# An adaLN attention block on one core: opening rebuilt around early loads and norms, and units of values placed between halves of the key products

## The chip, the cores and the metric
The kernel runs on one core of one Trainium2 chip. The metric is device time in microseconds (us), the median of the runs shown. The core has a matrix engine (PE, its weight loads shown as PEld), a vector engine (DVE), an activation engine (ACT), a general engine (POOL), a queue engine (SP) that issues nearly all transfers, and 16 DMA engines.

## The reference
One adaptive layer-norm block on x of 2048 rows by 512, all float32: attention with 32 heads of 16, then a Mish feed-forward of width 1792.

```python
mod = (_silu(c) @ w_mod).reshape(c.shape[0], 6, 1, -1)
sa, ca, ga, sb, cb, gb = (mod[:, 0], mod[:, 1], ...)
h = _layernorm(x) * (1 + ca) + sa
x = x + ga * _A_ref(h, A_wqkv, A_wo)      # softmax attention, 32 heads
h = _layernorm(x) * (1 + cb) + sb
x = x + gb * _B_ref(h, B_w1, B_b1, B_w2)  # dense, mish, dense
```

What this change touches is the way to the first `h` and to keys, queries and values: x is normalised, scaled by `1 + ca` and shifted by `sa`, and multiplied by `wqkv`.

## The kernel before
The order of all engines is written out by hand. Every product is made of three: each operand is split into a high part (rounded to the matrix engine's fast float32 form) and a low part (the rest), and high by high, high by low and low by high are added up in PSUM. `hi_copy` makes the high part, `lo_sub` the low one.

The work falls into an opening, four blocks of early projections, a lead-in of 20 steps, 512 steps of attention (32 groups of four heads and 512 queries, 16 steps each), with the feed-forward of earlier rows beside them, and a tail.

- Opening. SP loads c, the first two slices of the modulation weights (`wma`, shift and scale, 1 MB each), four tiles of x (128 rows each), the first 128 columns of the key and query weights (`wr`), then the rest of x and the value weights. POOL fills constants. `sil` is silu(c). Sums over c are matrix products whose left operand is `sil`, one slice of 128 rows to a strip of 32 output rows; a second product with `sel` adds the four strips and turns them into columns (`modc`). `first_norm` takes mean and variance of x tiles 0 to 3 on DVE and the root on POOL; `first_apply` normalises them; `first_tr` transposes them on PE into four PSUM banks.
- Blocks. A block `tb` is 512 rows. `stats_tb` (DVE, POOL) and `apply_tb` (ACT) normalise its four tiles, `tr_tb` transposes them and makes, for each of four k, `h_h` (ACT, high part), `hf` (DVE, full value, after ACT has read the bank) and `h_l` (the difference: on DVE for the k in `LOV[tb]`, else on POOL). The first key product (`qk_unit(1, 0, tb)`) starts with eight products on `h_h` ("early") and ends with four on `h_l` ("late"); block 0 has the query product too. Its result is split by ACT (`qh`) and DVE (`ql`) and stored. In blocks 1 and 2, all eight early products are followed by two units of values (`v_unit`: 12 products of 256 columns for 128 rows); then come block `tb + 1`'s transposes of two k, the late products, and the transposes of the other two.
- Banks. PSUM has a ring of six banks and two more (`ms`, `acc`). `ring()` hands out the next bank; whoever writes it waits for those that read its former contents.
- Lead-in. Step t from -20 to -1 takes two pairs of maxima (`max_pair`: four products of 64 rows on `ka` and `qa`, two DVE reductions of 1024) and then as many products of the queue of units as `CREDIT` allows; one credit is one product of 512 columns. `plan` lists the units: values of the first half, then query and key projections. What is left at step 0 goes beside the scores.

One PE queue, one DVE queue and so on run strictly in the order written.

## Time and profile before

| | us |
|---|---|
| median of 3 runs | 1693.89 (1693.4 to 1694.09) |
| profiled execution | 1694.02 |
| its span | 1692.1 |
| busy PE / DVE / ACT / POOL | 1671.4 / 1442.0 / 1354.5 / 821.1 |
| first x tile ready (start of its statistics) | 9.76 |
| first product of block 0 (PE, L131) | 19.95 |
| first maxima (lead-in starts) | 50.29 |
| first score (step 0) | 103.31 |

Times inside the execution are from the start of the span. A timeline row has start, duration, engine, line, operation, tiles (written, then read), shapes, count, and in brackets the idle time before it and what ended it. A stretch row has its length, then for each engine busy us and, as (x…), the instructions, then the granted PE clock (1.00 is full), the DMA share and GB/s. Rows with one count over several instructions merge them.

### The profile page before, as it was taken

To read this page: it belongs to the slowest core of one execution; us is meant where nothing else is said; L and a number is where in the kernel's file an instruction comes from. 1 tells how busy PE (TensorE), PEld (TensorE's weight loads), DVE (VectorE), ACT (ScalarE), POOL (GpSimd) and SP (SyncE) were. 2 spreads that over 40 slices of the span, in tenths; PEclk is the share of its full clock that TensorE was granted. 3 is DMA by queue.
4 is the path that set the end of the run, shared out by engine and by line. 5 is a ranking of instruction groups with operands and counts; after the bars stand their busy time and mean duration, and the time that the engine had idled before them with its cause. 6 is when DMAs were issued, how large, how long until landed. Compare 5 with 4: busy or idle time off the path is not lost.

```text
span 1692.1 us, 33739 instructions
## 1 busy us (share of the span) xinstructions
PE 1671.4 (99%) x12410; PEld 925.8 (55%) x12410; DVE 1442.0 (85%) x2371; ACT 1354.5 (80%) x2610; POOL 821.1 (49%) x843
## 2 busy tenths in 40 slices
PE   7999999999999999999999999999999999999999
PEld 5755665555444555555555455555555455555587
DVE  8888888888889888888889888888889888884377
ACT  6257777777778988888888998888888998888674
POOL 7556224665413564555323564555323565555443
PEclk9999999999999999999999999999999999999999
DMA  7877545777755343434355434424354533533261
GB/s 250 260 239 201 132 136 179 229 224 216 216 172 142 106 101 84 127 80 131 85 145 148 118 74 97 137 73 132 82 146 126 131 93 77 143 107 128 77 230 63
DMA packets 114029, 238.44 MB, mean 141 GB/s; under 512 B 23824, under 2 KB 49424, under 8 KB 107912
## 3 DMA queue, kind: packets, MB, share of 16 engines
q1 hardware_dynamic: 113864, 236.28, 49.5%
q8 instruction: 98, 1.61, 0.4%
q14 instruction: 67, 0.55, 0.1%
HBM read 179.95 MB, written 51.44 MB: 137 GB/s over the span
## 4 chain that ended last, share of the span: by engine, by line
PE 92%; DVE 3%; ACT 3%; DMA 1%; issue 1%; POOL 1%; SPq 0%; ACTq 0%; DVEq 0%; POOLq 0%
PE bk L605 29%; PE ring L587 22%; PE ring L538 20%; PE bk L138 10%; PE bk L131 3%; PE ring L131 2%; PE ring L1214 2%; DVE mx L540 2%; ACT pr L590 1%; PE ring L552 1%; DMA xt<-in_A_x 0%; PE ring L917 0%; PE ring L567 0%; PE ring L138 0%; DMA ka<-kscr 0%
## 5 line engine op out<-in xcount | busy, mean ns | idle before, releaser
L540 DVE TENSOR_REDUCE mx<-ring 128x1 f32<-128x512 f32 x1968 | 1222.9, 683 | 151.3 <-PE ring L538 137.9
L590 ACT ACTIVATE pr<-ring 128x512 f32<-128x512 f32 x2048 | 1078.3, 603 | 209.3 <-PE bk L138 116.4
L538 PE MATMUL ring<-ka,qa 64*128 64x512 f32 x1968 | 818.6, 429 | 1.3 <-ACT pr L590 1.1
L587 PE MATMUL ring<-qa,ka 64*128 64x512 f32 x2048 | 759.4, 402 | 2.2 <-ACT pr L590 2.0
L605 PE MATMUL bk<-pr,vg 128*32 128x512 f32 x4096 | 545.1, 605 | 0.0
L538 PEld LDWEIGHTS ring<-ka,qa 64*128 64x128 f32 x1968 | 350.8, 184 | 326.2 <-DVE mx L540 251.3
L587 PEld LDWEIGHTS ring<-qa,ka 64*128 64x128 f32 x2048 | 374.0, 184 | 193.1 <-DVE mx L540 112.2
L138 PE MATMUL bk<-h,w 64*128 64x512 f32 (+1 forms) x1080 | 278.1, 391 | 0.0
L138 PE MATMUL bk<-w,a_h 64*128 64x512 f32 x632 | 211.0, 413 | 0.0
L138 PEld LDWEIGHTS bk<-h,w 64*128 64x128 f32 x1080 | 178.8, 185 | 8.4 <-ACT pr L590 1.5
L605 PEld LDWEIGHTS bk<-pr,vg 128*32 128x32 f32 x4096 | 80.8, 108 | 136.1 <-issue 126.6
L138 PE MATMUL bk<-w,a_l 64*128 64x512 f32 x316 | 124.3, 393 | 0.0
L138 PEld LDWEIGHTS bk<-w,a_h 64*128 64x128 f32 x632 | 106.9, 185 | 3.9 <-ACT hb L795 0.8
L973 POOL TENSOR_TENSOR y<-yd,y 128x512 f32<-128x512 f32 x44 | 56.9, 1292 | 89.1 <-ACT yd L972 84.2
L807 POOL TENSOR_SCALAR qq<-ee 128x512 f32<-128x512 f32 x25 | 15.5, 619 | 169.3 <-ACT ee L801 169.3
L823 POOL TENSOR_TENSOR qq<-qq,rr 128x512 f32<-128x512 f32 x42 | 54.2, 1289 | 86.0 <-ACT rr L817 86.0
L809 POOL TENSOR_TENSOR hb<-hb,ee 128x512 f32<-128x512 f32 x42 | 54.1, 1289 | 79.6 <-DVE ee L805 77.7
L138 PE MATMUL bk<-w,o_hl 64*128 64x512 f32 x288 | 79.1, 405 | 0.0
L100 POOL TENSOR_TENSOR a_l<-hb,a_h 128x512 fp32r<-128x512 f32 x53 | 73.2, 1381 | 4.4
L138 PEld LDWEIGHTS bk<-w,a_l 64*128 64x128 f32 x316 | 58.4, 185 | 3.2
L97 POOL TENSOR_SCALAR qh<-qf 128x512 fp32r<-128x512 f32 x27 | 16.7, 620 | 88.9 <-ACT qf L261 75.2
L138 PE MATMUL bk<-h_h,wl 64*128 64x512 f32 x168 | 57.2, 420 | 0.2 <-ACT pr L590 0.2
(222 smaller groups left out, 1917.0 us busy)
## 6 DMA issues: line engine op xcount, KB each, us to landing
ka<-kscr SPq DMA_DIRECT2D x124, 384.0 KB
w<-w2scr SPq DMA_DIRECT2D x56, 512.0 KB
w<-w1scr SPq DMA_DIRECT2D x46, 512.0 KB
vg<-vscr SPq DMA_DIRECT2D x32, 552.0 KB
qa<-qscr SPq DMA_DIRECT2D x124, 100.0 KB
kscr<-qh SPq DMA_DIRECT2D x16, 512.0 KB
qscr<-qh SPq DMA_DIRECT2D x32, 256.0 KB
w2scr<-hl SPq DMA_DIRECT2D x14, 512.0 KB
```

The source lines that it names most:

```text
L100: (nc.gpsimd if eng == "p" else nc.vector).tensor_sub(lo, src, hi.bitcast(F32))
L131: nc.tensor.matmul(acc, l, r, start=start, stop=stop)
L138: i = nc.tensor.matmul(acc, l[64 * g:64 * g + 64], r[64 * g:64 * g + 64], start=start and not then, stop=bool(stop and then))
L538: nc.tensor.matmul(pm, qt[64 * s:64 * s + 64, qs * P:(qs + 1) * P], kt[64 * s:64 * s + 64, kb * TB:(kb + 1) * TB], start=True, stop=True)
L540: nc.vector.tensor_reduce(out=mxs[n][:, s, 4 * j + qs, kb:kb + 1], in_=pm, op=ALU.max, axis=AX.X)
L587: nc.tensor.matmul(p_, kt[64 * s:64 * s + 64, kc * P:(kc + 1) * P], qt[64 * s:64 * s + 64, :], start=True, stop=True)
L590: e = nc.scalar.activation(pr, p_, AF.Exp, scale=SCALE)
L605: nc.tensor.matmul(accs[n][32 * h:32 * h + 32, :], vgs[n][:, o:o + 32], pts.pop((t, h)), start=(kc == 0), stop=(kc == 15))
L809: (nc.vector if tail else nc.gpsimd).tensor_mul(hb, hb, ee)
L823: nc.gpsimd.tensor_mul(qq, qq, rr)
L973: nc.gpsimd.tensor_add(y[i], yd, y[i])
L1214: nc.tensor.matmul(po[i // 2][:, i % 2, :], l[:, s], w[:, r, :], start=(f == 0 and j == 0), stop=(f == FT - 1 and j == 2))
```

## The change
Loads: c comes by ACT's queue, ahead of ACT's table load. SP loads x tiles 0 to 3, the shift's weights in four slices, x tiles 4 to 7, key weights, the scale's weights in four slices, query and value weights, the rest. POOL no longer fills the two `ka` tiles with ones; ACT copies them. `sel` is gone.

Opening: the statistics and applies of tiles 0 to 7 stand ahead of block 0, in pairs; tile 3 is applied on POOL, the rest on ACT. The sums run slice by slice, in an output of 32 equal rows per 128 columns, and one transpose turns a copy of it into columns. 66 transposes of the identity into an unused bank (`keep_busy`) stand among them. DVE makes the low part of the key weights and the high part of the query weights, and POOL the low part of the latter.

Blocks: in blocks 1 to 3 the early key products come in two halves, each followed by one unit of values, so six units instead of four are done here. `plan` starts at unit 6, and `CREDIT` is 6.65 instead of 7.2.

```diff
-    CREDIT = 7.2
+    CREDIT = 6.65
...
+    nc.scalar.dma_start(cc, c.rearrange("o (k p) -> p (o k)", p=P))
     nc.scalar.preload_act_table_set("natural_log_exp_and_others")
...
-        wma = [lp.tile([P, DK, D], F32, name=f"wma{i}") for i in range(2)]
-        for i in range(2):
-            nc.sync.dma_start(wma[i], w_mod[:, i * D:(i + 1) * D].rearrange("(k p) m -> p k m", p=P))
+        wma = [[lp.tile([P, D], F32, name=f"wma{i}{k}") for k in range(DK)] for i in range(2)]
+
+        def load_mod(i):
+            for k in range(DK):
+                nc.sync.dma_start(wma[i][k], w_mod[k * P:(k + 1) * P, i * D:(i + 1) * D])
+
         for t in range(4):
             load_x(t)
-        slice_load(1, 0, lp, lp)
-        slice_load(0, 0, lp, lp)
+        load_mod(0)
         for t in range(4, 8):
             load_x(t)
+        slice_load(1, 0, lp, lp)
+        load_mod(1)
+        slice_load(0, 0, lp, lp)
         slice_load(2, 0)
...
-        for i in range(2):
-            nc.gpsimd.memset(ka[i].bitcast(F32), 1.0)
+        hi_copy("a", ka[0], ones.to_broadcast([P, S]))
+
+        spare = ring()
+
+        def keep_busy(n):
+            for _ in range(n):
+                nc.tensor.transpose(spare[:, :P], ident, ident)
+
+        keep_busy(40)
...
+        def mod_sums(i, ks):
+            for k in ks:
+                for m in range(DK):
+                    nc.tensor.matmul(prs[i][32 * m:32 * m + 32, :P], sil[:, k:k + 1].to_broadcast([P, 32]),
+                                     wma[i][k][:, m * P:(m + 1) * P], start=(k == 0), stop=(k == DK - 1))
+
+        def mod_cols(i):
+            row = lp.tile([P, P], F32, name=f"row{i}")
+            nc.vector.tensor_copy(row, prs[i][:, :P])
+            nc.tensor.transpose(prs[i][:, P:2 * P], row, ident)
+            cols = prs[i][:, P:2 * P:32]
+            if i:
+                nc.vector.tensor_scalar_add(modc[:, i, :], cols, 1.0)
+            else:
+                nc.vector.tensor_copy(modc[:, i, :], cols)
...
+        for q in range(2):
+            stats_two(q)
+        first_apply(3, "p")
+        for q in range(2, 4):
+            stats_two(q)
+        mod_sums(0, (0, 1))
+        keep_busy(6)
+        first_apply(0)
+        first_tr(0)
+        mod_sums(0, (2,))
+        first_apply(1)
+        first_tr(1)
+        mod_sums(0, (3,))
+        first_apply(2)
+        first_tr(2)
+        first_tr(3)
+        keep_busy(12)
+        mod_cols(0)
+        hi_k = split_hi(1, 0, "a")
+        for i in range(4, 8):
+            first_apply(i)
+        for k in range(DK):
+            mod_sums(1, (k,))
+            keep_busy(1)
+        mod_cols(1)
+        split_lo(1, 0, hi_k, "v")
+        hi_q = split_hi(0, 0, "v")
+        split_lo(0, 0, hi_q, "p")
+        keep_busy(4)
+        tr_tb(0, pts=pts)
...
-            pe_queue.extend(m for e in early for m in e)
-            pe_run()
-            if tb in (1, 2):
-                for kc in (2 * tb - 2, 2 * tb - 1):
-                    unit(v_unit(0, kc, "ring"))
+                pe_queue.extend(m for e in early for m in e)
+                pe_run()
+            else:
+                for i in range(2):
+                    pe_queue.extend(early[0][j + k] for k in (2 * i, 2 * i + 1) for j in (0, DK))
+                    pe_run()
+                    unit(v_unit(0, 2 * tb - 2 + i, "ring"))
...
-    plan = [(-PRO, 2, 0, range(4, 16)), (-PRO, 0, 1, (0,)), (-PRO, 1, 1, range(NB)), (-PRO, 1, 2, range(NB)),
+    plan = [(-PRO, 2, 0, range(6, 16)), (-PRO, 0, 1, (0,)), (-PRO, 1, 1, range(NB)), (-PRO, 1, 2, range(NB)),
```

DVE's queue between the statistics and the first `hf` of block 0, before (the apply of tile 3, the columns, four pairs of statistics of block 1, of which the first and last stand here, and the first `hf`):

```order
L419 TENSOR_SCALAR xt_140<-xt_140,ln_rs4_189 128x512
L462 TENSOR_SCALAR modc_95<-bk_212 128x4
L463 COPY modc_95<-bk_212 128x4
L373 BN_STATS ln_st_247<-xt_146 128x6
L374 BN_AGGR ln_mv4_245<-ln_st_247 128x2
...
L373 BN_STATS ln_st_256<-xt_152 128x6
L374 BN_AGGR ln_mv4_245<-ln_st_256 128x2
L440 TENSOR_SCALAR hf_281<-ring_100,modc_95 128x512
```

and in the changed kernel, from the last statistics of block 1 on:

```order
L399 BN_STATS ln_st_278<-xt_150 128x6
L400 BN_AGGR ln_mv2_273<-ln_st_278 128x2
L439 COPY row0_338<-ring_96 128x128
L445 COPY modc_91<-ring_96 128x4
L439 COPY row1_368<-ring_96 128x128
L443 TENSOR_SCALAR modc_91<-ring_96 128x4
L98 TENSOR_TENSOR wl_372<-wr_152,wh_342 128x512
L93 CAST wh_374<-wr_158 128x512
L458 TENSOR_SCALAR hf_382<-ring_96,modc_91 128x512
```

The statistics of block 1 stand ahead of the columns now, and behind the columns stand two splits of weights.

PE's queue in block 1 before (`wh` on the right of the arrow first: values; `h_h` first: key products):

```order
L131 MATMUL ring_100<-h_h_117,wh_200 128x512 x4
L131 MATMUL ring_100<-h_h_117,wl_235 128x512 x4
L131 MATMUL ring_100<-wh_325,h_h_117 128x256 x4
L131 MATMUL ring_100<-wl_326,h_h_117 128x256 x4
L131 MATMUL ring_100<-wh_325,h_l_118 128x256 x4
```

and in the changed kernel, from the last product of the first half:

```order
L129 MATMUL ring_96<-h_h_113,wl_372 128x512
L129 MATMUL ring_96<-wh_422,h_h_113 128x256 x4
L129 MATMUL ring_96<-wl_423,h_h_113 128x256 x4
L129 MATMUL ring_96<-wh_422,h_l_114 128x256 x4
L129 MATMUL ring_96<-h_h_113,wh_342 128x512
```

The first unit of values has moved ahead of the last four early products.

SP's queue at the start before (c, the two slices of modulation weights, x):

```order
L331 DMA cc_128<-in_c 128x4x1
L341 DMA wma0_130<-in_w_mod 128x4x512
L341 DMA wma1_131<-in_w_mod 128x4x512
L336 DMA xt_134<-in_A_x 128x512
L336 DMA xt_136<-in_A_x 128x512
```

and in the changed kernel, from the last tile of the first four on:

```order
L332 DMA xt_138<-in_A_x 128x512
L339 DMA wma00_124<-in_w_mod 128x512
...
L332 DMA xt_150<-in_A_x 128x512
L231 DMA wr_152<-in_A_wqkv 128x4x128
L339 DMA wma10_128<-in_w_mod 128x512
L339 DMA wma11_129<-in_w_mod 128x512
L339 DMA wma12_130<-in_w_mod 128x512
```

x now leads, and the scale's weights stand behind eight tiles of x.

More of the change, by code (lines that the diff above doesn't have):

```diff
@@ L74, in adaln_block @@
     nc.gpsimd.memset(ones, 1.0)
-    sel = cst.tile([P, 1], F32, name="sel")
-    nc.gpsimd.memset(sel, 0.0)
-    for k in range(DK):
-        nc.gpsimd.memset(sel[32 * k:32 * k + 1, :], 1.0)
     lows = cst.tile([P, 1], F32, name="lows")
@@ L329, in adaln_block @@
         lp = es.enter_context(tc.tile_pool(name="lp", bufs=1))
-        cc = lp.tile([P, DK], F32, name="cc")
-        nc.sync.dma_start(cc, c.rearrange("o (k p) -> p (o k)", p=P))
         xts = []
@@ L363, in adaln_block @@
         nc.vector.tensor_mul(sil, cc, e)
+        hi_copy("a", ka[1], ones.to_broadcast([P, S]))
         rss = {}
@@ L441, in tr_tb @@
                 lo_sub("v" if k in LOV[tb] else "p", h_l[:, k, s], hf, h_h[:, k, s])
[L443 to L466 removed]
+        for q in range(2):
[19 more added lines that the diff above has]
+            first_apply(i)
+        for k in range(DK):
+            mod_sums(1, (k,))
[6 more added lines that the diff above has]
+        tr_tb(0, pts=pts)
         def constants():
```

85 lines of the change are left out of this document (27 added, 58 removed).

## The prediction
> **What bounds the kernel now.** I read the stretches of the span first, then the timeline of the opening.
>
> ```profile
> core 0: us, PE busy (x) PEld busy (x) DVE busy (x) ACT busy (x) POOL busy (x), PEclk, DMA share, GB/s
> 0.00:16.20 16.20, 7.00 (x32) 4.02 (x33) 10.47 (x14) 5.30 (x8) 12.14 (x36) 1.00 0.91 317
> 16.20:50.29 34.09, 31.64 (x174) 25.15 (x175) 30.75 (x53) 24.17 (x37) 21.29 (x25) 1.00 0.66 218
> 50.29:56.83 6.54, 6.54 (x38) 5.42 (x38) 4.95 (x5) 1.85 (x4) 5.21 (x4) 0.74 0.62 224
> 56.83:103.31 46.48, 46.36 (x263) 32.57 (x262) 42.81 (x40) 7.97 (x19) 24.66 (x25) 1.00 0.90 278
> 103.31:1588.00 1484.69, 1479.57 (x11428) 778.30 (x11429) 1276.51 (x2155) 1258.42 (x2456) 720.92 (x716) 1.00 0.49 132
> ```
>
> From 103.31, where the first scores start, PE is busy 1479.57 of 1484.69 us, and no row of the change lies behind that point except one product; the order of every engine there is the old one. So the change is worth what it moves the moment 103.31. Ahead of it lie three stages: loads and norms (to 16.2, PE mostly waiting), four blocks of early projections (to 50.29, DVE busy 30.75 of 34.09) and 20 lead-in steps of maxima and units (to 103.31, PE full).
>
> ```profile
> 1.23 1.04 SPq L341 DMA_DIRECT2D wma<-in_w_mod  x2
> 2.31 2.14 SPq L336 DMA_DIRECT2D xt<-in_A_x  x4
> 3.18 5.55 DVE L361 TENSOR_SCALAR sil_e<-sil_e 128x4 f32<-128x4 f32 x1 [1.53 <-ACT sil_e L360]
> 9.76 0.69 DVE L394 BATCH_NORM_STATS2 ln_st<-xt 128x6 f32<-128x512 f32 x1 [0.61 <-DMA xt<-in_A_x]
> 11.21 0.59 ACT L452 COPY row<-ring 128x512 f32<-128x512 f32 x1 [8.05 <-PE ring L448]
> 12.91 0.59 ACT L452 COPY row<-ring 128x512 f32<-128x512 f32 x1 [1.12 <-PE ring L448]
> 16.54 0.15 DVE L463 COPY modc<-bk 128x4 f32<-128x4 f32 x1
> 16.61 0.68 DVE L373 BATCH_NORM_STATS2 ln_st<-xt 128x6 f32<-128x512 f32 x1
> 19.84 0.81 DVE L440 TENSOR_SCALAR hf<-ring,modc 128x512 f32<-128x512 f32 x1
> 21.40 0.69 DVE L100 TENSOR_TENSOR h_l<-hf,h_h 128x512 fp32r<-128x512 f32 x1
> 22.11 3.78 POOL L100 TENSOR_TENSOR h_l<-hf,h_h 128x512 fp32r<-128x512 f32 x3
> 22.19 2.93 ACT L384 ACTIVATE xt<-xt,ln_rs 128x512 f32<-128x512 f32 x4 [0.38 <-POOL ln_rs L378]
> 27.78 0.81 DVE L440 TENSOR_SCALAR hf<-ring,modc 128x512 f32<-128x512 f32 x1
> ```
>
> The first x tile waits behind 2 MB of modulation weights until 9.76. The modulation columns are there at 16.7, but DVE then takes statistics of block 1 and reaches the first `hf` at 19.84; block 1's first `hf` comes 7.94 us later.
>
> **Loads and norms.** x goes first. The last slice of modulation weights is then the 17th piece of 256 KB where the first x tile was the 9th. Pieces come at the rate of this row:
>
> ```profile
> 9.20:20.00 10.80, 10.63 (x49) 7.33 (x49) 7.94 (x20) 4.79 (x8) 5.75 (x12) 1.00 1.07 395
> 25.03 1.03 ACT L93 CAST wh<-wr 128x1024 fp32r<-128x1024 f32 x1
> 15.00 2.68 POOL L100 TENSOR_TENSOR wl<-wr,wh 128x512 fp32r<-128x512 f32 x2
> 15.07 1.47 DVE L419 TENSOR_SCALAR xt<-xt,ln_rs 128x512 f32<-128x512 f32 x1 [2.02 <-POOL ln_rs L399]
> ```
>
> Eight more pieces are 2.1 MB, 5.3 us at 395 GB/s; the queue starts 0.5 us earlier: 9.7 + 5.3 - 0.5 = 14.5. Then a sum, 0.4 (a quarter of the 12.91 less 11.21 that a sum of all four slices took), a copy, 0.3 (between 0.15 and 0.59), a transpose, 0.3, and an add, 0.15: columns at 15.7, by these bounds 15.3 to 16.2.
>
> What I cost at nothing: eight weight loads for two add six issues on SP, which stay beside data that is slower (a piece takes 0.66 us); without that cover each costs its issue, some 0.5. c on ACT's queue adds an issue there, and the two fills of `ka` come from POOL, some 2 us each (twice the 1.03 us row). Both lie inside the 8.05 us in which ACT waited; behind them stand only Exp and the first applies. Without that cover the columns stay and the applies come up to 4 us later. POOL without the fills frees DVE, which stood 5.55 us at 3.18, so `sil` no longer comes at 9.14. The apply of the fourth tile on POOL takes at most a POOL subtraction's 1.3 us, before 12, with POOL's norm chains of tiles 4 to 7 behind it and these due only at 15.7. The sums with `sel` go and 66 transposes come, on a PE that had 7.00 busy of 16.20.
>
> The statistics of block 1 took 3.2 us (16.61 to 19.84). They and their applies are now done by 15.7, since twelve pieces are in by 9.7 + 2.0 - 0.5 = 11.2. So DVE goes from the columns to the key weights' low part (0.69, as the `h_l` row) and the query weights' high part (0.45, between 0.15 and 0.69) and starts `hf` at 16.9, 2.9 us ahead of 19.84. The 2.93 us of ACT at 22.19 leave the block, where DVE and not ACT is late.
>
> Part of the lead is given back. DVE's subtraction at 21.40 took 0.69 us with POOL not yet at its `h_l`; the apply at 15.07 stood 1.2 us until POOL's subtraction ended. Now POOL has no norm chain to do there: after the query weights' low part (17.0 to 18.3) it goes straight to `h_l`, and DVE, asking at 18.4, waits 1.2 us. Lead: 1.9, at best 2.9.
>
> **Units of values between the halves.** Block 2 in the trace:
>
> ```profile
> 36.88 1.28 POOL L100 TENSOR_TENSOR h_l<-hf,h_h 128x512 fp32r<-128x512 f32 x1
> 37.05 1.66 DVE L100 TENSOR_TENSOR h_l<-hf,h_h 128x512 fp32r<-128x512 f32 x1
> 38.63 0.68 DVE L100 TENSOR_TENSOR ql<-ring,qh 128x512 fp32r<-128x512 f32 x1
> 39.37 0.53 PEld L131 LDWEIGHTS ring<-wh,h_h 128*128 128x128 f32 x4 [0.37 <-DVE ql L100]
> 42.35 0.60 PE L434 MATMUL ring<-ident,xt 128*128 128x128 f32 x4
> 43.87 0.81 DVE L440 TENSOR_SCALAR hf<-ring,modc 128x512 f32<-128x512 f32 x1 [1.91 <-ACT h_h L439]
> 46.51 0.68 DVE L100 TENSOR_TENSOR ql<-ring,qh 128x512 fp32r<-128x512 f32 x1
> ```
>
> A unit's bank is the one that block 1's key product leaves, so the first unit of a block waits for `ql` (39.37, 0.37 us). Before, all eight products stood ahead of it; now the last four stand behind it on PE's queue, and so do the transposes of block 3. `ql` is ready 1.7 us earlier (DVE again behind POOL's `h_l`, as at 37.05) to 3.1 us earlier (DVE asks first, since its `hf` no longer waits): unit at 37.7 to 36.2. I take 36.2, because DVE's request then falls before POOL's norm chain is through. PE idles 1.4 us for it. From there: unit 1.49 (39.37 to 42.35 are two), four products 0.95, unit 1.49, so transposes at 40.1. `ql` of block 2 ends 4.84 us after its transposes (47.19 less 42.35), at 45.0; PE is there at 43.7 and idles 1.3 us. Then unit, products, unit, late products: 4.87. The lead-in starts at 49.8, 0.5 us ahead of 50.29, with two units more done. Bounds 48.8 and 51.3.
>
> **Lead-in.**
>
> ```profile
> 47.76:51.17 3.41, 2.31 (x10) 0.96 (x9) 2.12 (x4) 0.73 (x2) 1.26 (x1) 1.00 1.01 363
> 51.17:54.58 3.41, 3.41 (x16) 3.17 (x17) 2.84 (x3) 0.75 (x2) 2.96 (x2) 0.50 0.34 112
> 23.86:27.27 3.41, 2.88 (x17) 2.13 (x15) 3.27 (x9) 3.41 (x5) 2.47 (x3) 1.00 0.45 19
> 57.49 0.74 PE L131 MATMUL bk<-wl,h_h 128*128 128x256 f32 x4
> 58.07 0.64 PE L131 MATMUL bk<-wh,h_l 128*128 128x256 f32 x4
> 58.55 0.64 PE L131 MATMUL bk<-wh,h_h 128*128 128x256 f32 x4
> L554 DVE TENSOR_REDUCE mx<-ring 128x2 f32<-128x1024 f32 x40 | 47.1, 1221 | 4.5 <-PE ring L552 3.7
> ```
>
> A credit is two half-wide products, 0.24 us (58.07 to 58.55 are four). 20 steps x 0.55 credits x 0.24 = 2.6 us less. Also the first two steps, 6.54 us, exceed two later ones (46.48 / 18 = 2.58 each) by 1.4: the clock was 0.50 for 3.41 us after a stretch of 3.41 us with 2.31 busy. A stretch with 2.88 busy had no such consequence. 53.02 - 2.6 - 1.4 = 49.0 on PE; DVE needs 40 x 1.22 + 0.6 = 49.4, part behind the first score: I take 49.3.
>
> Sum: 49.8 + 49.3 = 99.1, or 4.2 us less than 103.31, at full clock. The two idle times, 1.4 and 1.3, leave between 2.0 and 2.7 busy of 3.41, astride 2.31 and 2.88: I count one halving, 1.4 us, as before. So -2.8 us. The profiled execution took 1694.02 us around its span of 1692.1, 0.13 above the median 1693.89; 1693.9 - 2.8 gives 1691.1, forecast 1691.0.
>
> The Trainium skill (TensorE: Matmul & The Clock Gate, "What's actually happening") halves the clock only after an idle window of about 3.4 us. This trace halves it after one that was 2.31 us busy, so here the row decides. By the page the change would have no halving: the first rival's time.
>
> **Rivals.**
> - *No halving.* Idle times fall across two stretches. For it: 2.88 busy of 3.41 was harmless; against: both waits together are 2.7 us in 9. -4.2 us: 1689.7; with DVE ahead of POOL in block 0 as well 1688.7.
> - *Two halvings, or the units only wait.* PE stops at both units for a bank, or DMA, at 0.90 share from 56.83 on, holds the shorter steps. -1.4 to 0 us: 1692.5 to 1694.
> - *Slower: the clock is still half in the opening.* These transposes were 0.22 us apart, later ones 0.11:
>
> ```profile
> 17.07 0.42 PE L426 MATMUL ring<-ident,xt 128*128 128x128 f32 x1
> 17.29 0.42 PE L426 MATMUL bk<-ident,xt 128*128 128x128 f32 x1
> 25.34 0.60 PE L434 MATMUL bk<-ident,xt 128*128 128x128 f32 x4
> ```
>
>   The granted clock reads 1.00 there, so the spacing is the evidence; and PE had run sums since 9.2. Of the 66 added transposes 62, and 17 others, stand ahead of the columns on PE: 79 x 0.215 = 17.0 us, and eight sums of 0.43, 3.4. From 1.6 on that is 22.0, columns at 22.8 instead of 15.7: 7.1 us late, +4.3 in all: 1698.2. It is slower from columns at 18.5 on. Against it: 40 transposes without a pause look like the full work that ended in 0.11 us spacing.
>
> **How the numbers follow.** One halving 0.38, none 0.28, two or held steps 0.14, cold opening 0.20. 0.2% is 3.4 us, about what a measurement of this kernel can tell from no change; the line is 1690.5. The forecast's own range is 1690.0 to 1692.5, from the bounds 48.8 and 51.3 of the lead-in's start, and 0.12 of its 0.38 lie past that line. Faster 0.28 + 0.12 = 0.40; slower 0.18, as a clock that comes up late but before the columns leaves 0.02 of its 0.20 within; within, the rest, 0.42. The range for all is 1688.0 to 1696.5. Below, the 1688.7 of the first rival, less 0.3 if the steps go at PE's 49.0 and 0.4 for columns at 15.3. Above, a cold opening that costs 5.4 of its 7.1 us.
>
> **What would show it.** Right: columns near 15.7, first `hf` near 16.9, `h_l` on DVE near 1.7 us long, PE idle until `ql` in blocks 2 and 3, the lead-in from 49 to 51.5, its steps 2.45 us, first score near 100.5. Wrong: transposes 0.22 us apart after 9 us, columns past 18, granted clock 0.50 for more than one stretch, or steps still at 2.58.

## The result, and the profile after

The changed kernel takes 1696.12 us (median of 22 runs, 1694.47 to 1698.0), the kernel before 1693.6 on the same chip (22 runs, 1692.6 to 1696.56). The ratio is 1.0014, with a 95% interval of 1.0008 to 1.002: about 2.4 us slower, where 2.8 us faster was forecast. That is less than the 0.2% which the prediction named as the bound, but the interval leaves out no change. The profiled execution took 1696.04 us around a span of 1693.9.

The same five stretches as before, for the changed kernel (length, then busy us and, as (x…), the instructions of PE, its weight loads, DVE, ACT and POOL, then granted clock, DMA share and GB/s):

```profile
0.00:16.20 16.20, 14.38 (x134) 11.86 (x134) 7.37 (x23) 10.74 (x12) 9.67 (x36) 1.00 0.90 299
16.20:50.29 34.09, 29.92 (x183) 25.17 (x184) 28.52 (x46) 22.16 (x35) 19.57 (x20) 0.95 0.70 223
50.29:56.83 6.54, 5.75 (x37) 4.12 (x36) 3.30 (x4) 1.85 (x4) 3.26 (x3) 1.00 0.64 228
56.83:103.31 46.48, 46.09 (x260) 32.03 (x261) 44.85 (x42) 7.71 (x17) 26.32 (x26) 1.00 0.91 278
103.31:1588.00 1484.69, 1477.42 (x11411) 775.44 (x11411) 1275.95 (x2154) 1258.00 (x2455) 719.70 (x716) 1.00 0.49 132
```

The halved clock has left the lead-in and sits in the blocks (0.95 over 34.09 us is one stretch of 3.4 us). The last row has PE busy 2.15 us less in the same time: behind the first score too, where the prediction counted nothing, time was lost.

The timeline of the opening and of block 0:

```profile
10.03 0.69 DVE L399 BATCH_NORM_STATS2 ln_st<-xt 128x6 f32<-128x512 f32 x1 [1.58 <-DMA xt<-in_A_x]
17.15 0.42 PE L434 MATMUL ring<-wma,sil 128*32 128x128 f32 x8 [1.29 <-DMA wma<-in_w_mod]
18.35 0.16 DVE L443 TENSOR_SCALAR modc<-ring 128x4 f32<-128x4 f32 x1 [0.42 <-PE ring L440]
19.38 0.81 DVE L458 TENSOR_SCALAR hf<-ring,modc 128x512 f32<-128x512 f32 x1
20.94 1.69 DVE L98 TENSOR_TENSOR h_l<-hf,h_h 128x512 fp32r<-128x512 f32 x1
28.30 0.80 DVE L458 TENSOR_SCALAR hf<-ring,modc 128x512 f32<-128x512 f32 x1
```

The last modulation slice lands at 17.15, not 14.5. So the first `hf` is 0.46 us ahead of the kernel before and not 2.9, DVE loses 1 us at `h_l` behind POOL, and block 1 starts half a microsecond behind it (28.30 against 27.78). Then the units of values, and the start of the lead-in:

```profile
38.48 0.74 PE L129 MATMUL ring<-wh,h_h 128*128 128x256 f32 x4 [1.16 <-DVE ql L98]
47.30 0.74 PE L129 MATMUL ring<-wh,h_h 128*128 128x256 f32 x4 [1.12 <-DVE ql L98]
52.24 0.73 PE L578 MATMUL ring<-ka,qa 64*128 64x512 f32 x3
53.75 0.50 PE L578 MATMUL ring<-ka,qa 64*128 64x512 f32 x1 [0.79 <-DVE ql L98]
```

PE waits at the units as forecast (1.16 and 1.12), and a third time for the same kind of bank at the second pair of maxima. The lead-in starts at 52.24, 1.95 later than before with two units more done, and lasts 50.18 instead of 53.02. So the first score comes 0.89 us earlier. What follows takes it back:

```profile
101.69 0.62 POOL L95 TENSOR_SCALAR qh<-qf 128x512 fp32r<-128x512 f32 x1 [4.70 <-DMA kscr<-qh]
102.42 0.47 PE L613 MATMUL ring<-qa,ka 64*128 64x512 f32 x1
103.71 0.59 ACT L259 COPY qf<-bk 128x512 f32<-128x512 f32 x1 [4.28 <-POOL ql L98]
104.19 2.07 ACT L616 ACTIVATE pr<-ring 128x512 f32<-128x512 f32 x4
110.59 1.07 PE L631 MATMUL bk<-pr,vg 128*32 128x512 f32 x8
```

And the kernel before at that place:

```profile
101.29 0.62 POOL L97 TENSOR_SCALAR qh<-qf 128x512 fp32r<-128x512 f32 x1 [3.47 <-DMA kscr<-qh]
103.97 2.07 ACT L590 ACTIVATE pr<-ring 128x512 f32<-128x512 f32 x4
110.36 1.06 PE L605 MATMUL bk<-pr,vg 128*32 128x512 f32 x8
```

`qh` and `ql` have two buffers each, and `qf`, the copy out of PSUM from which POOL makes them, has one. POOL waits 4.70 us until a store of keys (`kscr<-qh`) has left a buffer of `qh`; ACT's next copy to `qf` waits for POOL; and the first exponentials (`pr`), which stand behind that copy on ACT's queue, start at 104.19, 0.22 us later than before although their scores were there 0.9 us earlier. The first product of probabilities with values is at 110.59 instead of 110.36. The store ends at nearly the same moment in both kernels (101.69 and 101.29); in the kernel before it was early enough for a first score at 103.31. Counted by the moments at which equally many of these products had started (the line's instructions up to a given time, to about 0.1 us), the changed kernel is 0.2 behind at 112 us, 0.5 at 370, 1.2 at 450, 1.4 at 900 and 1.7 at 1580. The one wait for a transfer that PE shows there is for `qa<-mt`, which puts the maxima into the operand of the scores:

```profile
385.33 0.46 PE L613 MATMUL ring<-qa,ka 64*128 64x512 f32 x1 [0.92 <-DMA qa<-mt]
```

### The profile page after: what moved, and what is told of

It reads as the page before. It is cut to its first block, busy times and chain, and to the rows that moved or that the text cites. A ratio compares the mean times of both kernels' runs of the same rounds, so it can differ in the third digit from the quotient of the medians.

```text
span 1693.9 us, 33942 instructions
## 1 busy us (share of the span) xinstructions
PE 1675.5 (99%) x12510; PEld 929.8 (55%) x12510; DVE 1436.6 (85%) x2374; ACT 1358.2 (80%) x2610; POOL 816.6 (48%) x839
## 4 chain that ended last, share of the span: by engine, by line
PE 90%; DVE 3%; DMA 2%; ACT 2%; POOL 1%; issue 1%; SPq 0%; ACTq 0%; POOLq 0%; DVEq 0%
PE bk L631 29%; PE ring L613 22%; PE ring L564 19%; PE bk L136 11%; PE bk L129 2%; PE ring L1240 2%; PE ring L129 2%; DVE mx L566 2%; ACT pr L616 1%; DMA kscr<-qh 0%; DMA qa<-mt 0%; PE ring L943 0%; DMA wma<-in_w_mod 0%; PE ring L593 0%; PE ring L578 0%
```

## The experiments

My theory after this reading, called the handover below: the lead-in is held at its end by its transfers, in the order in which its steps issue them, and an earlier first score is spent there. Among these transfers are stores and loads of keys, queries and values, and six slices of the feed-forward's first weights, which are loaded, split on POOL and stored again. What the changed kernel's DMA view counts between 50 and 112 us:

```profile
DMA packets 13364, 17.41 MB, mean 281 GB/s; under 512 B 893, under 2 KB 8117, under 8 KB 13167
```

The rivals: the opening itself costs the time, or the units between the halves do. All runs in one table; "hold" is the time from the first score to the first product of probabilities with values, ratios are against the kernel before on the same chip, and the moments are those of one profiled execution. That execution need not be a median one: those of e1, e2 and g2 took 2.5, 3.0 and 3.7 us more than the median of their runs, those of g4 and h2 1.7 and 1.3 less.

| run | first `hf` | lead-in | first score | first product with values | hold | ratio (95%) |
|---|---|---|---|---|---|---|
| before | 19.84 | 50.29 | 103.31 | 110.36 | 7.05 | |
| after | 19.38 | 52.24 | 102.42 | 110.59 | 8.17 | 1.0014 (1.0008 to 1.002) |
| e1 opening alone | 19.39 | 49.73 | 102.62 | 110.68 | 8.06 | 1.0004 (0.9996 to 1.0013) |
| e2 units alone | 19.81 | 51.58 | 103.32 | 113.28 | 9.96 | 1.0006 (0.9997 to 1.0015) |
| e3 weights first | 21.58 | 56.46 | 107.69 | 115.38 | 7.69 | 1.0036 (1.0023 to 1.0049) |
| e5 three slices | 19.29 | 52.15 | 102.24 | 109.27 | 7.03 | 1.0116 (1.0102 to 1.013) |
| f1 after, slices forward | 19.35 | 52.20 | 102.29 | 109.35 | 7.06 | 1.0001 (0.9992 to 1.001) |
| f2 before, slices forward | 19.93 | 50.38 | 101.91 | 108.98 | 7.07 | 0.9993 (0.9984 to 1.0002) |
| f3 scale weights whole | 23.00 | 55.86 | 106.28 | 116.32 | 10.04 | 1.0037 (1.0023 to 1.0051) |
| f4 lows on POOL | 19.27 | 50.83 | 101.83 | 110.29 | 8.46 | 1.0014 (1.0004 to 1.0024) |
| g1 f1 and f4 | 19.61 | 52.39 | 102.46 | 109.53 | 7.07 | 0.9999 (0.999 to 1.0008) |
| g2 e2, slices forward | 20.17 | 51.96 | 102.93 | 112.97 | 10.04 | 1.0 (0.9991 to 1.0009) |
| g3 e1, slices forward | 19.49 | 50.04 | 101.56 | 108.63 | 7.07 | 0.9996 (0.9987 to 1.0005) |
| g4 g1 and key low part early | 19.25 | 50.37 | 100.45 | 107.54 | 7.09 | 0.9992 (0.9983 to 1.0001) |
| h1 after, PE kept busy | 19.59 | 52.45 | 102.95 | 111.01 | 8.06 | 1.0015 (1.0006 to 1.0024) |
| h2 g4 and h1 | 19.44 | 50.58 | 100.65 | 107.71 | 7.06 | 0.9988 (0.998 to 0.9997) |
| h3 h2 and block 2's lows | 19.57 | 49.98 | 100.05 | 109.58 | 9.53 | 0.9992 (0.9983 to 1.0001) |
| i1 after again | 19.71 | 52.56 | 103.44 | 111.55 | 8.11 | |
| i2 before again | 20.13 | 50.57 | 102.07 | 110.21 | 8.14 | |

### The two parts alone

Run e1 takes the units and credits of the kernel before into the changed one:

```diff
-    CREDIT = 6.65
+    CREDIT = 7.2
...
+            pe_queue.extend(m for e in early for m in e)
+            pe_run()
+            if tb in (1, 2):
+                for kc in (2 * tb - 2, 2 * tb - 1):
+                    unit(v_unit(0, kc, "ring"))
...
-    plan = [(-PRO, 2, 0, range(6, 16)), ...
+    plan = [(-PRO, 2, 0, range(4, 16)), ...
```

> The changed kernel's loads, norms and sums, but units of values as in the kernel before (two units behind all eight early products in blocks 1 and 2, plan from unit 4, CREDIT 7.2). Theory (handover): the first `hf` comes near 19.4 as in the changed kernel, the first score between 102 and 103.3, and the first product of probabilities with values still at 110.4 to 110.7, since transfers fill the time from 56 to 115; the time is that of the kernel before within 1.5 us. Rival (units): the units between the halves are what makes the change slow; then this kernel is 0.5 to 2 us faster than before. Rival (opening): the late modulation weights and the halved clock in block 0 make it slow; then it is as slow as the changed kernel, +2.5 us.

Run e2 is the reverse: the kernel before with the halves, `range(6, 16)` and 6.65.

> The kernel before with the units of values between the halves, six of them, plan from unit 6 and CREDIT 6.65; loads and norms as before. Theory (handover): lead-in from about 52.5, first score 102 to 103, first product of probabilities with values 110.4 to 110.7: nothing of an earlier first score is left there; time 0 to +2 us on before. Rival (opening): without the changed opening the units give what the lead-in saves, -0.9 us or better. Rival (units): +2.5 us as the whole change.

Neither part alone is told from the kernel before (+0.04% and +0.06%, both intervals take in 1). Nor do these times settle which half costs the 2.4 us: the intervals reach +2.2 and +2.5 us. The moments say more. The first score of e1 is where expected, that of e2, 103.32, just past the expected 103, and both runs stand at a transfer there: e1 waits 1.31 us for `qa<-mt` and reaches the first product with values at 110.68, inside the expected 110.4 to 110.7. e2 missed that: 113.28. The timeline of e2, and its stretch:

```profile
103.32 0.46 PE L589 MATMUL ring<-qa,ka 64*128 64x512 f32 x1 [1.57 <-DMA qa<-mt]
113.28 1.07 PE L607 MATMUL bk<-pr,vg 128*32 128x512 f32 x8
104.00:112.00 8.00, 6.87 (x31) 4.39 (x29) 5.60 (x9) 5.35 (x11) 2.30 (x3) 0.57 0.95 313
```

Behind PE's pauses at the first scores the clock was 0.57 over 8 us. So a halved clock came on top of the hold's own 1 us in this execution; in that of e1, which waited 1.31 us, it did not.

### Transfers at the end of the lead-in

Run e5 leaves three of the six weight slices out of the lead-in, to follow with the later ones:

```diff
-    EARLY = 6
+    EARLY = 3
```

> The changed kernel with three instead of six slices of the feed-forward's first weights loaded, split and stored in the lead-in (the other three join those that follow later); 2.3 MB of the 17.4 MB that move between 50 and 112 leave. Theory (handover): the waits of POOL's `qh` for the stores of keys (6.5 us in the changed kernel) shrink, the first score stays near 102.4, the first product of probabilities with values comes at 109.5 to 110.0 instead of 110.6, and the time falls by 0.6 to 1.1 us, unless the moved slices cost it again later. Rivals (opening, units): transfers are not what takes the 0.9 us; the first product with values stays at 110.6.

Run f1 leaves nothing out and asks for the six slices sooner; f2 does the same to the kernel before:

```diff
-        at(3 * i - 37, lambda i=i: early_prep(i, 3 * i - 37))
+        at(2 * i - 39, lambda i=i: early_prep(i, 2 * i - 39))
```

> The changed kernel with the six early slices of the feed-forward's first weights asked for every second half-step from -39 on instead of every third from -37; nothing is left out or added, PE, DVE and ACT keep their order. Theory (the lead-in is now shorter at both ends, and its 17 MB of transfers are tied to its steps, so that they and not the products set its end): with transfers brought forward the wait for the stores of keys before step 0 shrinks, the first score stays at 102.0 to 102.6, the first product of probabilities with values comes at 109.3 to 110.2 (110.6 in the changed kernel), and the time falls by 0.4 to 1.3 us. Rival: the wait for stores is only a matter of POOL's queue (its splits stand ahead of `qh`); then moving splits forward changes the first product with values by under 0.2.

> The kernel before with the same move of the six slices. Theory: its lead-in has 2.8 us more for the same transfers, and its first product of probabilities with values stood 7.05 after the first score, as it stands in the changed kernel when transfers do not hold it (109.27 - 102.24 = 7.03 with three slices less); so nothing is to be won: first score 103.3, first product with values 110.2 to 110.5, time within 0.5 us of before. Rival: if transfers bind both kernels alike, it wins the same 0.4 to 1.3 us as the changed kernel with this move.

The timeline of f1:

```profile
102.29 0.49 PE L613 MATMUL ring<-qa,ka 64*128 64x512 f32 x1
102.96 2.07 ACT L616 ACTIVATE pr<-ring 128x512 f32<-128x512 f32 x4
109.35 1.06 PE L631 MATMUL bk<-pr,vg 128*32 128x512 f32 x8
```

With the order of PE, DVE and ACT unchanged and the same bytes moved, the first score stays (102.29 against 102.42) and the first product with values comes 1.24 us earlier; the ratio falls from 1.0014 to 1.0001 (the two intervals just overlap). In e5 it came 1.32 earlier. POOL's wait for the store ended at 99.84 in f1 and 99.56 in f2, where it was 101.69 in the changed kernel. The rival, that only POOL's queue matters, allowed under 0.2; and POOL stood idle in that wait. So the handover holds. Since e5 and f1 both move work of POOL with the transfers, what speaks for the transfers is the releaser that the rows name. (e5's time itself is 20 us longer: PE waits 6.68 us for an operand of the feed-forward, and its busy time between 1580 and 1640 falls from 60.00 to 51.69; that the slices left to later make it late is my reading. It says nothing on the handover.) f2 went by its rival: the kernel before has as much to win, 1.38 us at the first product with values. I had reckoned that it had slack; it has none. By time f2 stands at 0.9993, f1 at 1.0001 on the same chip: with the transfers forward in both kernels, the change still gains nothing that these runs can tell.

### The loads of the opening

Run e3 loads both sets of modulation weights and the key weights ahead of x tiles 4 to 7:

```diff
         load_mod(0)
+        load_mod(1)
+        slice_load(1, 0, lp, lp)
         for t in range(4, 8):
             load_x(t)
-        slice_load(1, 0, lp, lp)
-        load_mod(1)
...
-        for q in range(2, 4):
-            stats_two(q)
         mod_sums(0, (0, 1))
...
+        for q in range(2, 4):
+            stats_two(q)
         tr_tb(0, pts=pts)
+        for i in range(4, 8):
+            first_apply(i)
```

> The changed kernel, but the scale's weights and the key weights are loaded ahead of x tiles 4 to 7, and the statistics and applies of these tiles stand where the kernel before has them, ahead of and behind block 0's `hf`. The last modulation slice is the 12th piece of 256 KB and not the 17th: columns near 15 (18.35 in the changed kernel), first `hf` near 16 to 19, as x tile 7 is the 17th piece and its statistics stand ahead of `hf` on DVE. If the order of loads sets the opening, the first `hf` moves with the later of the two. Theory (handover): whatever the first score wins, the first product of probabilities with values stays at 110.4 to 110.7 and the time within 1 us of the changed kernel. Rival (opening): the time falls by what the first `hf` wins.

Run f3 loads the scale's weights in one piece:

```diff
-        load_mod(1)
+        nc.sync.dma_start(whole, w_mod[:, D:2 * D].rearrange("(k p) m -> p k m", p=P))
```

> The changed kernel with the scale's modulation weights in one transfer of 1 MB instead of four slices of 256 KB. If the four slices' own issue and the transfers that run beside them make the last one late (17.15 in the changed kernel), the sums start earlier, columns at 16.0 to 17.5 instead of 18.35. If bytes alone set it, the whole megabyte lands at 17.0 to 17.2, four sums follow instead of one, about 0.6 each, and the columns come at 19.5 to 20.5. Theory (handover): in both cases the time moves by under 1.5 us.

The timeline of PE in e3, with two rows of DVE:

```profile
12.48 1.47 PE L362 MATMUL ring<-ident 128*128 128x128 f32 x12
13.79 0.27 PE L440 MATMUL ring<-ident,row 128*128 128x128 f32 x1
15.84 0.42 PE L434 MATMUL ring<-wma,sil 128*32 128x128 f32 x8
17.05 0.16 DVE L443 TENSOR_SCALAR modc<-ring 128x4 f32<-128x4 f32 x1 [0.42 <-PE ring L440]
21.58 0.78 DVE L458 TENSOR_SCALAR hf<-ring,modc 128x512 f32<-128x512 f32 x1
```

The columns came 1.3 us sooner, at 17.05, not near 15: with the weights there, PE's own order is the limit, twelve fillers (the transposes of `keep_busy`) and then four sums with a filler each (0.61 us a slice, the last sum at 15.84). And statistics ahead of `hf` on DVE cost 3.3 us there (`hf` at 21.58, past the expected 16 to 19), and the lead-in starts 4.2 us later; my "within 1 us" was wrong, since the hold gave back only 0.5 of that. In f3 the megabyte landed 0.27 us after the last of the four slices had:

```profile
17.42 0.66 PE L436 MATMUL ring<-wma,sil 128*32 128x128 f32 x8 [3.25 <-DMA wma<-in_w_mod]
```

So bytes set that moment, not the number of transfers. The four sums then ran at half clock, 1 us each, and the columns came at 21.98, later than both expectations. The time missed too: 1.0037 beside 1.0014 is 3.9 us more than the changed kernel, not under 1.5, and the first product with values came 5.7 us later. With slices the sums of the first three are done while the last one lands; the columns were 3.6 us sooner.

### What sets block 0

Run f4 changes one entry, run h1 adds 16 fillers:

```diff
-    LOV = ((1,), (), (1, 3), (1, 3))
+    LOV = ((), (), (1, 3), (1, 3))
```

> The changed kernel with all four low parts of block 0 on POOL, none on DVE. DVE no longer stands 1.69 us at 20.94 behind POOL's subtraction: block 0's third `hf` comes at 20.9 to 21.1 instead of 22.55. POOL's four subtractions run 20.8 to 26.0 instead of three to about 25. Block 1's first `hf` at 26.5 to 27.5 instead of 28.30 if DVE's wait is what gives the lead back; at 28 or later if the wait of block 0's late products for POOL's fourth subtraction takes its place. Time: within 1 us of the changed kernel by the theory of the handover, since the lead-in's end is set by transfers.

```diff
         for k in range(DK):
+            if k == DK - 1:
+                keep_busy(10)
             mod_sums(1, (k,))
...
-        keep_busy(4)
+        keep_busy(10)
         tr_tb(0, pts=pts)
```

> The changed kernel with 16 more transposes of the identity on PE where it waits in the opening: ten ahead of the last sum (whose weights land at 17.15), six more behind the columns' transpose. Sums and columns keep their moments if the fillers end before the data arrive. The granted clock then stays 1.00 at 18 to 24. Theory (the port that DVE and POOL share, not PE's clock, sets block 0): block 1's first `hf` stays at 28.2 to 28.4, the lead-in at 52.1 to 52.3 and the time within 1 us of the changed kernel's 1696.1. Rival (the halved clock costs what it is long for, 1.7 us): lead-in at 50.5 to 51, time near 1694.5.

The changed kernel's stretches around the halved clock:

```profile
15.80:19.40 3.60, 1.53 (x16) 0.84 (x15) 1.34 (x5) 1.55 (x3) 0.00 (x0) 1.00 1.08 362
19.40:22.80 3.40, 3.40 (x8) 2.72 (x9) 3.37 (x5) 2.87 (x4) 2.53 (x2) 0.51 1.05 384
```

And in h1:

```profile
15.80:19.40 3.60, 3.19 (x31) 2.54 (x31) 1.12 (x4) 1.50 (x3) 0.00 (x0) 1.00 1.07 360
19.40:22.80 3.40, 3.40 (x17) 2.57 (x15) 3.37 (x5) 3.09 (x5) 2.54 (x2) 1.00 1.05 384
```

The fillers keep the clock at 1.00, and nothing moves: the lead-in at 52.45 (52.24), the ratio 1.0015. Block 0 is not set by PE. It is set by DVE, as f4 shows; its timeline:

```profile
20.71 0.80 DVE L458 TENSOR_SCALAR hf<-ring,modc 128x512 f32<-128x512 f32 x1
26.70 0.80 DVE L458 TENSOR_SCALAR hf<-ring,modc 128x512 f32<-128x512 f32 x1
101.83 0.47 PE L613 MATMUL ring<-qa,ka 64*128 64x512 f32 x1 [0.85 <-DMA qa<-mt]
110.29 1.06 PE L631 MATMUL bk<-pr,vg 128*32 128x512 f32 x8
```

Without DVE's subtraction the third `hf` is 1.84 us sooner, block 1's 1.60, the lead-in 1.41. At the first product with values 0.30 of it is left, and the ratio is the changed kernel's, 1.0014. That is the plainest case of the handover: 1.4 us won, and nothing of it in the ratio.

### The causes taken away together

g1 joins f1 and f4. g2 and g3 are e2 and e1 with the slices brought forward. g4 is g1 with one line moved, h2 is g4 with the fillers, h3 is h2 with block 2's low parts on POOL as well (`LOV = ((), (), (), (1, 3))`). The line moved in g4:

```diff
+        split_lo(1, 0, hi_k, "v")
         mod_cols(1)
-        split_lo(1, 0, hi_k, "v")
```

> The changed kernel with both edits of the runs before: the early slices brought forward, and block 0's low parts all on POOL. Theory (transfers hold the end of the lead-in; with them brought forward the blocks' lead arrives): lead-in from 50.8, first score at 100.8 to 101.2 without a wait for transfers, first product of probabilities with values at 107.8 to 108.4, time 1.0 to 1.6 us below the run with the slices brought forward alone (1694.1), or 1692.5 to 1693.1. Rival (later waits take it back whatever comes earlier): first product with values as above, but the time stays at 1694 to 1696.

> The kernel before with the units between the halves (six units, CREDIT 6.65) and the slices brought forward. Theory: lead-in from 51.6, first score near 101.7 without the 1.57 us wait for `qa<-mt`, no halved clock at 104 to 112, first product with values near 108.8, time 1692.6 to 1693.6, against 1694.8 for the units alone and 1693.1 for the kernel before with the slices brought forward. Rival (units between the halves cost by themselves): 1694.5 or more here too.

> The changed opening with the units and CREDIT of the kernel before, and the slices brought forward. Theory: lead-in from 49.7, its steps 2.58 us, first score near 101.3 without the 1.31 us wait for `qa<-mt`, first product with values near 108.3, time 1692.3 to 1693.4. Rival (the opening costs by itself, in a clock that is halved in block 0 or later): 1694.5 or more.

> As the first of these, and the key weights' low part is made on DVE ahead of the scale's columns, in the 3.4 us in which DVE waits for the sums, instead of behind them. First `hf` 0.69 us earlier, at 18.6 to 18.7; lead-in from 50.1 to 50.4 if block 0 passes it on, at 50.8 if POOL's subtractions or the query weights set block 0; first score at 100.2 to 100.5 or 100.9. Theory: the time falls by what the first score wins, 0 to 0.7 us, below the first of these.

> The fillers together with the three edits of the fastest version so far (slices brought forward, block 0's low parts on POOL, the key weights' low part ahead of the columns; 1693.0, where runs with the clock at 1.000 took 1691.6 and those at 0.999 took 1693.6). Theory: with the opening's clock kept up the lead-in starts at 50.2 to 50.5 in nearly every execution, the first score comes at 100.3 to 100.6, the first product of probabilities with values at 107.4 to 107.7, median 1691.3 to 1692.2, 1.4 to 2.3 us below the kernel before. Rival (the clock in the opening is not what parts those runs): median 1692.7 to 1693.3 as without the fillers.

> As the run ahead of it, and block 2's low parts all on POOL too, where DVE's subtraction took 0.69 in one execution and 1.71 in another. If that wait is what makes the blocks' lead differ by 1.4 us between executions, the lead-in starts at 49.5 to 50.4 and the median falls by up to 0.7 us; if POOL's fourth subtraction then sets block 2's late products, the lead-in starts at 50.6 to 51.2 and the median rises by 0.3 to 0.8 us.

g3 came within 0.4 us of what was expected: first score 101.56 without a wait, first product with values 108.63, 1693.14 us. g2 did not: it still waits 0.77 us for `qa<-mt`, then stands at half clock for some 3 us, and reaches 112.97; its median, 1694.03, lies between the two expectations. g1 missed (lead-in at 52.39, 1693.34 us). Its profiled execution lost f4's lead again, most of it in block 2, where DVE's subtraction stands behind POOL's:

```profile
36.29 1.71 DVE L98 TENSOR_TENSOR h_l<-hf,h_h 128x512 fp32r<-128x512 f32 x1
```

In f4 and in the changed kernel the same instruction took 0.69. Which of the two engines starts first there changes with the lead. In g4 the first `hf` did not come sooner, since it waits for ACT's `h_h` once DVE is free:

```profile
19.25 0.81 DVE L458 TENSOR_SCALAR hf<-ring,modc 128x512 f32<-128x512 f32 x1 [0.52 <-ACT h_h L457]
```

but the lead-in started at 50.37 and the first score at 100.45. h2 has the lowest ratio:

```profile
100.65 0.49 PE L615 MATMUL ring<-qa,ka 64*128 64x512 f32 x1
107.71 1.07 PE L633 MATMUL bk<-pr,vg 128*32 128x512 f32 x8
```

Its median is 1693.29 us (11 runs) beside 1694.46 for the kernel before (27 runs), ratio 0.9988 (0.998 to 0.9997): faster than the kernel before by 0.12%, some 2 us (1.2 by the medians), of the 2.65 us that its first product with values is ahead; the changed kernel's interval lies wholly above 1. Of fifteen runs h2 is the only one whose interval lies below 1, and that interval overlaps those of g4 and f2. f2 is the kernel before with the slices forward and nothing else, so how much of the 2 us is the change's own is not shown. By the median its expectation was missed and the rival's range met (1692.7 to 1693.3); that the clock of the opening does not part the runs, h1 says too. h3 reaches its lead-in and its first score soonest of all (49.98 and 100.05) and loses the lead at the handover, with the slices already brought forward and a halved clock behind it; its median, 1693.55, did not fall below h2's:

```profile
102.11 2.07 ACT L618 ACTIVATE pr<-ring 128x512 f32<-128x512 f32 x4
109.58 1.06 PE L633 MATMUL bk<-pr,vg 128*32 128x512 f32 x8
```

### Each kernel once more

Runs i1 and i2 are the changed kernel and the kernel before, unedited, one execution each (1697.75 and 1693.52 us, too few to compare).

> The changed kernel, unedited, in another execution. If the reading of its first profile holds: columns near 18.3, lead-in near 52.2, first score 102.2 to 102.9, wait of POOL's `qh` for stores of keys of 3 us or more before step 0, first product of probabilities with values 110.3 to 111.0. The wait of 0.92 us for `qa<-mt` at 385 comes again if it is a fixed consequence, and differs in place or size if it hangs on how transfers happen to fall.

> The kernel before, unedited, in another execution. If the halved clock at 51 to 54.6 belongs to this kernel: lead-in 50.3, first score 103.2 to 103.4, first product with values 110.3 to 110.5. If it comes and goes: no halved stretch, first two steps 2.5 us apart, first score near 101.9, first product with values 109 to 110.4, depending on whether transfers then hold the end of the lead-in.

The timeline of i2:

```profile
101.32 0.62 POOL L97 TENSOR_SCALAR qh<-qf 128x512 fp32r<-128x512 f32 x1 [4.73 <-DMA kscr<-qh]
102.07 0.50 PE L587 MATMUL ring<-qa,ka 64*128 64x512 f32 x1
103.83 2.07 ACT L590 ACTIVATE pr<-ring 128x512 f32<-128x512 f32 x4
110.21 1.06 PE L605 MATMUL bk<-pr,vg 128*32 128x512 f32 x8
```

In this execution of the kernel before the clock was not halved. Its first score came 1.24 us sooner than in the first one, and its first product with values 0.15. So the 1.4 us of the halved clock, which the forecast counted as a term, comes and goes, and between these two executions it was worth next to nothing: when PE is faster, the store of keys holds the same moment (101.32 here, 101.29 there). i1 had the long store wait (5.2 us), the first score at 103.44 and the first product with values at 111.55, past the expected 102.9 and 111.0, and the later waits again, in other sizes: 1.4 us for `qa<-mt` and 0.4 for `ka<-kscr` between 370 and 460 (0.9 in the first execution).

## Why the prediction was wrong

**Where it failed.** The step is "So the change is worth what it moves the moment 103.31". Its ground, that every engine's order is the old one from there on, is true. But the queue of transfers is behind by then, and it does not start anew at the first score. Stores of keys that the lead-in's steps issue set when `qh`'s buffers come free, and through POOL and ACT's queue when the first exponentials start. The hold from first score to first product with values is 7.03 to 7.09 us where transfers let go, and 7.7 to 8.5 where they don't (9.5 to 10 with a halved clock). In the kernel before it was 7.05 in the execution whose first score a halved clock had made late; in i2, without the halving, it was 8.14. Of the ten executions in the table with all six slices at their old places, that one alone has a hold under 7.6; of the eight with the slices forward, six have 7.06 to 7.09. The prediction had the parts of this in hand, a DMA share of 0.90 in that stretch, and read it as a rival that leaves "-1.4 to 0 us", at 0.14. It looked for lengthened steps. The steps were not lengthened (17 of them take 41.63 us between DVE's reductions at 56.48 and 98.11, 2.45 each as forecast); the bill came behind them, where it had declared the cost nil.

**The whole sum.** The forecast's first score is at 100.5 (49.8 + 49.3 + 1.4). It came at 102.42: the lead-in's start 2.4 us late, the lead-in 0.9 longer, and 1.4 less because no halving fell into it. So 0.89 was left of the 2.8. The hold took 1.1 more than in the kernel before, and the rest of the attention 1.4; so at 1580 the changed kernel is 1.7 us late. The late start is the largest term, and the prediction knew its price: it called the change slower "from columns at 18.5 on", and they were there at 18.51. But f4 and f1 show that neither repair alone is enough: the lead-in 1.4 sooner without the transfers left the ratio at 1.0014, the transfers without the lead-in brought 1.0001, and where both came together, in the profiled executions of g4 and h2, the spans are 1689.4 and 1690.1 against 1692.1 (by the medians of their runs the lead is 0.5 and 1.2 us).

**What it was measured against.** Set beside i2, the changed kernel's first score is not ahead at all: 102.42 and, in i1, 103.44 against 102.07. Of the 2.84 us by which its lead-in is shorter (50.18 against 53.02), 1.52 belong to the halved clock in the first execution of the kernel before; i2 took 51.50. The 1.3 that are left are less than the 1.67 by which its lead-in starts later than that of i2 (50.57).

**Above zero.** The rival at 0.14 could not explain a loss, and nothing in the forecast's range of causes did but a cold opening. Of the 1.8 us in the span, 0.2 are there at 110 us. Some 0.7 come between 370 and 450, where one wait for a transfer took 0.92 (in i1 waits of 1.8, and 1.9 us came there). The rest, some 0.9, is spread with no wait that PE shows. PE waited for transfers between 370 and 460 in both executions of the changed kernel and in neither of the kernel before; of the other 15 runs in the table, 11 have such waits, of 0.2 to 1.8 us, and e3, f1, g4 and h2 have none. Why the changed kernel meets them stays open. SP took 4.40 and 4.80 us there for the four issues of `qa<-mt` in its two executions, 3.12 and 3.52 in those of the kernel before; but f4 waited 0.36 behind issues of 2.87. That f1 had no wait fits an easier queue, but f2, with the same move, had one of 0.43.

**Columns at 15.7.** The add that ends them started at 18.35, so they were there at 18.51. The 17th piece landed at 17.15 instead of 14.5; what follows it, 1.15 in the forecast, took 1.36. The ninth piece of 256 KB, from which the other eight were counted, was 0.8 us late already (10.03 instead of 9.2). The other 1.8 us come from taking the stretch's full rate for pieces in strict order. The rows from 0, and from the ninth piece, to the landing of the 17th:

```profile
0.00:17.15 17.15, 14.38 (x135) 11.86 (x135) 7.37 (x23) 11.04 (x12) 9.67 (x36) 1.00 0.91 302
10.03:17.15 7.12, 5.69 (x69) 3.77 (x61) 3.49 (x10) 4.30 (x6) 3.24 (x9) 1.00 1.08 356
```

302 GB/s in 17.15 us are 5.18 MB; 17 pieces are 4.46 MB. So some 0.7 MB, nearly all of it later pieces of the same queue, had moved ahead of it. Behind the ninth piece, 356 GB/s instead of 395 cost 0.6 us for eight pieces, and bytes of later ones the other 1.2. The Trainium skill (DMA: Bandwidth & Descriptors, "Queues, rings and completion order") says that completion is not in order for one issuing engine. This trace agrees as far as bytes go, by that 0.7 MB; which of the later pieces completed first, its rows do not show.

**Given back behind POOL's `h_l`.** Right, in mechanism and size: 1.69 us at 20.94, 1.0 more than the 0.69 before, where 1.2 was forecast. With a lead of 0.46 and not 2.9 it left block 1 half a microsecond behind.

**Units of values.** PE's waits were forecast at 1.4 and 1.3 and measured 1.16 and 1.12. Their place was not: 38.48 instead of 36.2, because of the late columns. A third wait for the same bank, 0.79 us at the second pair of maxima, was not seen. The lead-in's start, 52.24, lies outside the bounds of 48.8 and 51.3.

**Lead-in.** 49.3 was forecast and 50.18 came; the third wait is 0.79 of the difference.

**One halving, 1.4 us.** One halving came, in block 0, and cost nothing (h1). The rule drawn from one window, that 2.31 us busy of 3.41 halves the clock and 2.88 does not, fell: the kernel before with the slices forward had the same stretch nearly to the digit and kept its clock.

```profile
47.76:51.17 3.41, 2.33 (x10) 0.97 (x9) 2.12 (x4) 0.64 (x2) 1.27 (x1) 1.00 0.98 347
51.17:54.58 3.41, 3.41 (x26) 2.92 (x27) 3.41 (x4) 0.84 (x2) 2.86 (x2) 1.00 0.39 135
```

The section cited beside it, of the Trainium skill (TensorE: Matmul & The Clock Gate, "What's actually happening"), lets an idle window halve the clock; the changed kernel's 15.8 to 19.4, with 1.53 of 3.60 us busy, was followed by a halved stretch, so page and row still differ there. It also calls the window free-running. That fits a stretch which halves in one execution and not in the next, though no run here shows where a window begins.

**The slower rival, a cold opening,** did not come: 40 transposes took 6.74 us from 1.34 on, and those of x behind 9.3 stood 0.11 us apart.

## What to carry to other kernels

An earlier start is worth what is left of it at the first point where compute and transfers meet again, so follow the gain past the last moved instruction to the next wait on a transfer, above all where the DMA share is over 0.9 on the way. Look at two executions before counting a clock event as a term: here a 1.24 us earlier first score in the unedited kernel was worth 0.15 us seven microseconds later. And when a stage is shortened, move its transfers forward with it: that alone brought the changed kernel from 1.0014 to 1.0001 here. Make the same move in the kernel before, too, ahead of judging the change: it stood at 0.9993 with it.

## What the runs showed that I had not expected

- In e2 and g2 a wait of PE of 1.6 and 0.8 us at the first scores was followed by a half clock for some 7 and 3 us (e2: 0.57 over 8 us), and the hold was about 10 us; it was 8.1 in e1, which had a wait of 1.31 and no halving. What decides between the two stays open.
- A halved clock cost nothing in block 0, where DVE sets the pace: 3.4 us at 0.51, and with the fillers that undid it the lead-in came 0.2 us later.
- DVE's subtraction of two SBUF tiles took 0.69 us or up to 1.71 in the same place of the same order, as POOL's subtraction started after or before it (0.07 us after in f4, 0.12 before in g1). A lead of a microsecond can so be spent at the next such meeting.
